# Attention fused with a two-layer MLP: the first pair of token blocks goes through the second weight by plain products

## The chip, the cores and the metric

The kernel runs on one NeuronCore of a Trainium2 chip. The core has a matrix engine (TensorE, in the profile PE, and PEld for its weight loads), three engines for elementwise work (VectorE or DVE, ScalarE or ACT, GpSimd or POOL), a SyncE (SP) that issues transfers, and 16 DMA engines. Every engine works through a queue of its own in program order and waits there for semaphores of the others. The metric is the time of one execution on the device in microseconds: the median of three runs before was 390.96 us (390.53 to 391.64).

## The reference

Softmax attention over 8 batches, 12 heads, 448 tokens, 64 elements a head, and then an MLP with a leaky rectifier over the 3,584 rows of 768 numbers:

```python
scores = scale * np.matmul(q, k.transpose(0, 1, 3, 2))
attn = np.exp(scores - np.max(scores, axis=-1, keepdims=True))
attn = attn / (np.sum(attn, axis=-1, keepdims=True) + 1e-09)
x = np.matmul(attn, v)           # to (3584, 768)
h = x @ w_in                     # w_in: 768 x 2048
g = np.maximum(0.01 * h, h)
out = g @ w_out                  # w_out: 2048 x 768
```

Inputs and output are float32; the kernel multiplies in bfloat16 and sums in float32.

## The kernel before, in words

**Attention.** The 48 pairs of heads (8 batches of 6) are numbered u = 0 to 47. For a pair, q, k and v are loaded by POOL's DMA queue (`load_soft`, L141), cast to bfloat16 (`cast`, L170 and L172, by POOL from u = 4 on), and q and k are transposed: by TensorE up to u = 14 (`transposes`, L254, with a copy by VectorE, L260), later by a DMA transpose on SP (`dma_transposes`, L237). Scores are made in four chunks of 112 keys a pair (L271, two matmuls a chunk), and ScalarE takes the exponential (L280). A *burst* is three chunks, one into each of three PSUM slots. When the four chunks of a pair are done, `rows` multiplies by v (32 matmuls, L765); VectorE then takes the reciprocal of the sums (L771) and multiplies (L772), and SP transposes the result into `xT` (L237). This step of pair u is called *row block u* below. It occupies one of the three slots until L772 has ended.

**MLP.** Tokens are cut into stages of 640, 512, 512, 512, 512, 384 and 512. A stage first makes h (`head` and `neck` for stage 0, `hidden(i)` for the others) and then the output (`second(i)`), two blocks of 128 tokens at a time. `head` takes the first 448 tokens by plain products, `neck` the next 192 (L621, with the rectifier on ScalarE, L648). `hidden` and `second` use Winograd's form of Strassen's scheme: seven products of half matrices in the place of eight, with sums of the operands made beforehand on VectorE and sums of the results afterwards.

**Sums of the operands.** `mix_weights` is a generator that makes the sums of w_out's quarters in four pieces: `t3` (L364) and `t2` (L366) and `t4` (L372) into `w_mix`, and L369, which replaces the right half of w_out's upper rows by right minus left, in place. A `next(outs)` emits one of the 16. Three are taken in `head`, 13 in `neck` by `after`. `mix_w_in` does the same for w_in; its last five steps (L390) are taken in `second(0)`, by `next(ins)`. `mix_h(i, m)` makes, for two of the upper eight row blocks of h, the difference of the two blocks of tokens of each pair into `h_mix` (L435) and adds the lower half of h to the upper half in the second block of the pair, in place (L436). For stage 0 its four calls stand in `after`, behind every second step of `neck`.

**A pair of blocks.** `block_pair(i, c)` is a generator too. It runs seven products of eight matmuls of 384 columns (L535), yielding in the middle of and after each, so that it has 14 steps, x = 0 to 13. Two PSUM banks, `banks`, are used in turn. VectorE sums h in place (L547, L552), copies a bank out (`keep`, L540) or adds it (`join`, L543), and SP stores the block (L330).

**Order of the work.** All of it is emitted in a fixed order, written out by hand. Between the steps of a pair, `place` decides by a clock of its own (`model`) whether a burst or a row block goes in: 0.65 us a half product, 0.78 a burst, 1.08 a row block, 0.8 an exponential; a slot is free when that clock has passed its due time. At steps 1 and 3 no row block is placed (`calm`), since the pair's first sums are then on VectorE. At even steps `advance` emits a DMA transpose of q and k (SP), a cast (POOL), a cast of v, and every second time a load. `plan` has nine bursts in `second(0)`. The sums of x for the next stage (L415) are emitted one a step from 7 us of that clock after the row block that they need, and what is left of them at the end of `second`. `second(0)` begins with 13 row blocks done and must end with 18; the first bursts take their chunks from u = 13.

Of the kernel before, what the change touches and what calls it, by code (L numbers as in the profile page):

```python
# [9 lines left out]
F32 = mybir.dt.float32  # L10
# [6 lines left out]
def kernel(  # L17
# [9 lines left out]
    nc = tc.nc  # L27

    B, H, S, D = q.shape
    DM, DF = moe_w_in.shape  # L30
    P = 128
# [4 lines left out]
    MD = DF // P  # L36
    NW = DM // 2
    NU = B * HP
# [3 lines left out]
    NR = len(cuts) - 1  # L42
    HEAD = S
    need = [HP * -(-t // S) for t in cuts]
# [14 lines left out]
    o_pool = ctx.enter_context(tc.tile_pool(name="o", bufs=3))  # L59
# [6 lines left out]
    banks = [ps_g.tile([P, 4 * P], F32, name=f"g{i}") for i in range(2)]  # L66
# [7 lines left out]
    def next_bank():  # L74

        banks.reverse()
        return banks[1]
# [17 lines left out]
    def place_of(t):  # L95
        return (t + NX - cuts[3]) % NX
# [6 lines left out]
    w_out_sb = w_pool.tile([P, MD, DM], BF16)  # L103
# [3 lines left out]
    h = h_pool.tile([P, MD, (KEEP + 1) * P], BF16, name="h")  # L107
    h_mix = h_pool.tile([P, MH, 2, P], BF16, name="hmix")
# [13 lines left out]
    for t in (w_in_mix, w_mix):  # L122
        t = t.rearrange("p x k n -> p (x k n)")
# [197 lines left out]
    def store(o, t0, cols=slice(0, DM), queues=(nc.sync, nc.sync)):  # L321

        queues = list(queues)
        done = 0
        while done < P:
            b, j = divmod(t0 + done, S)
            so, p = divmod(j, SC)
            n = min(SC - p, P - done)
            dst = out[b * S:(b + 1) * S].rearrange("(p so) n -> so p n", so=NSC)
            queues.pop(0).dma_start(out=dst[so, p:p + n, cols], in_=o[done:done + n, cols])  # L330
            done += n
# [4 lines left out]
    def settle(n=3):  # L336
        while late and n:
            expo(*late.pop(0))
            n -= 1
# [4 lines left out]
    def part(i, m, kks, bank=None):  # L344

        n = HEAD
        at = place_of(0)
        fresh = m not in open_t
        if fresh:
            open_t[m] = next_bank() if bank is None else bank  # L350
        for kk in kks:
            nc.tensor.matmul(
                open_t[m][:, :n], w_in_sb[:, kk, ts(m, P)], xT[:, kk, at:at + n],
                start=(fresh and kk == kks[0]), stop=(kk == KD - 1),
            )

    def mix_weights():

        pieces = [(slice(m, m + 2), slice(MH + m, MH + m + 2)) for m in range(0, MH, 2)]
        left, right = slice(0, NW), slice(NW, DM)  # L360
        for todo in (pieces[:2], pieces[2:]):
            for lo, hi in todo:
                t2, t3 = w_mix[:, 0, lo], w_mix[:, 1, lo]
                nc.vector.tensor_sub(t3, w_out_sb[:, hi, right], w_out_sb[:, lo, right])  # L364
                yield
                nc.vector.tensor_add(t2, t3, w_out_sb[:, lo, left])  # L366
                yield
            for lo, hi in todo:
                nc.vector.tensor_sub(w_out_sb[:, lo, right], w_out_sb[:, lo, right], w_out_sb[:, lo, left])  # L369
                yield  # L370
            for lo, hi in todo:
                nc.vector.tensor_sub(w_mix[:, 2, lo], w_out_sb[:, hi, left], w_mix[:, 0, lo])  # L372
                yield

    def mix_w_in():

# [41 lines left out]
    def spots(i):  # L418

        if i == 0:  # L420
            return 0, [(0, 1), (2, 3)]
        return 0, [(0, 2), (1, 3)] if cuts[i + 1] - cuts[i] == 4 * P else [(0, 1), (KEEP, 2)]

    def token(i, x):

        return KEEP * P if x == KEEP else cuts[i] + x * P

    def mix_h(i, m):

        at = spots(i)[1]  # L430
        step = [max(1, at[-1][y] - at[0][y]) for y in range(2)]
        one, two = (slice(at[0][y], at[-1][y] + 1, step[y]) for y in range(2))
        lo, hi = slice(m, m + 2), slice(MH + m, MH + m + 2)
        t = h.rearrange("p m (c t) -> p m c t", t=P)
        nc.vector.tensor_sub(h_mix[:, lo, :len(at)], t[:, lo, one], t[:, lo, two])  # L435
        nc.vector.tensor_add(t[:, lo, two], t[:, lo, two], t[:, hi, two])  # L436

    def hidden(i):
# [79 lines left out]
    def block_pair(i, c):  # L518
# [67 lines left out]
        store(o2, t0)  # L586
        banks.reverse()

    def head(ins, outs):

        for m in opened:
            part(0, m, (KD - 1,))
        for m in range(MD):
            if m not in opened:
                part(0, m, range(KH))
                for _ in range(2 if 5 <= m < 11 else 0):
                    next(ins)
                for _ in range({13: 1, 15: 2}.get(m, 0)):
                    next(outs)
                yield KH * HEAD / 2400, False  # L600
                part(0, m, range(KH, KD))
            nc.scalar.activation(h[:, m, :HEAD], open_t.pop(m)[:, :HEAD], AX.Prelu, alpha=0.01)
            settle()
            if m == opened[-1]:
                slots.append(idle)
            yield (KH if m not in opened else 1) * HEAD / 2400, True

    def neck(outs):

        n = cuts[1] - HEAD  # L610
        at = place_of(HEAD)
        ms = [x + y for x in range(0, MH, 2) for y in (0, MH)]
        held = {}

        def part2(m, kks):
            fresh = m not in held
            if fresh:
                held[m] = next_bank()
            for j in range(2):
                for kk in kks:  # L620
                    nc.tensor.matmul(  # L621
                        held[m][:, j * n:(j + 1) * n], w_in_sb[:, kk, ts(m + j, P)], xT[:, kk, at:at + n],
                        start=(fresh and j == 0 and kk == 0), stop=(kk == KD - 1), skip_group_check=True,
                    )

        assert all(u == need[1] - 1 for u, _ in owed_x), owed_x
        def after(x):
            for _ in range((4, 4, 3, 2, 0, 0, 0, 0)[x]):
                next(outs)
            if x % 2:  # L630
                mix_h(0, ms[x - 1])

        for m in ms[:2]:
            part2(m, range(KD - 1))
        yield 4 * (KD - 1) * n / 2400, False
        for x, m in enumerate(ms):
            if x < 2:
                assert rows_done >= need[1], rows_done
                settle_x()
                part2(m, (KD - 1,))  # L640
                if x:
                    after(x - 1)
            else:
                part2(m, range(KH))
                after(x - 1)
                yield 2 * KH * n / 2400, False
                part2(m, range(KH, KD))
            nc.scalar.activation(  # L648
                h[:, m:m + 2, HEAD:cuts[1]], held.pop(m)[:, :2 * n].rearrange("p (m t) -> p m t", m=2), AX.Prelu, alpha=0.01
            )  # L650
            settle(1)
            yield 2 * (KH if x > 1 else 1) * n / 2400, True
        model["free"][id(slots[0])] = model["now"] + 1.5
        transposes(NPE - 1, next_slot()[:, 0])
        after(len(ms) - 1)

    def supply(u):
# [246 lines left out]
    def second(i):  # L904

        x_sums = [mix_x_part(i + 1, slice(0, 2)), mix_x_part(i + 1, slice(2, 3))] if i + 1 < NR else []
        fresh, summed = [None, None], [i + 1 == NR] * 2
        left = plan[i]
        for c in range(len(spots(i)[1])):
            for x, _ in enumerate(block_pair(i, c)):  # L910
                if x % 2 == 0:
                    advance()
                if c or x:
                    model["now"] += 0.65
                left -= place(i, left, calm=x not in (1, 3), keen=need[min(i + 2, NR)], cap=NU if all(summed) else need[i + 2])
                if i == 0 and x % 2:
                    next(ins, None)
                for y in range(2):
                    if fresh[y] is None and i + 1 < NR and rows_done >= need[i + 2] - 1 + y:
                        fresh[y] = model["now"] + 7.0  # L920
                for y, todo in enumerate(x_sums):
                    if fresh[y] is not None and fresh[y] <= model["now"] and not summed[y]:
                        summed[y] = next(todo, 0) is not None
                        if not summed[y]:
                            break
        assert left == 0 or chunk == NU * NSC, (i, left)
        assert i + 1 == NR or rows_done >= need[i + 2], (i, rows_done)
        for todo in x_sums:
            for _ in todo:
                pass  # L930

    ins, outs = mix_w_in(), mix_weights()
# [60 lines left out]
```

## Time and profile before

| | |
|---|---|
| three runs, median (lowest to highest) | 390.96 us (390.53 to 391.64) |
| the profiled execution, its own time | 392.0 us |
| its span, first to last instruction | 390.1 us |
| mean granted clock of TensorE | 0.994 |
| `neck`, by TensorE | 62.8 to 73.5 us |
| `second(0)`, by TensorE | 73.9 to 109.4 us |
| first matmul of `hidden(1)` | 110.1 us |

Times in the profile are microseconds from the first instruction, durations of one form in ns. A line of the timeline gives start, duration, engine, line, operation, what it writes and reads, and how often; brackets give how long the engine stood idle before and what ended that. A duration of a merged group of matmuls includes the pipeline's depth, so groups overlap by some 0.15 us: the start of the next group tells the pace.

### The profile page before, as it was taken

What the parts mean: (1) busy time and instruction counts of PE and PEld (TensorE: products, weight loads), DVE (VectorE), ACT (ScalarE), POOL (GpSimd) and SP (SyncE); (2) the same over time, 40 slices, a digit from 0 to 9 for tenths busy, and PEclk for the clock granted to TensorE, in tenths of its full rate; (3) what the DMA queues carried; (4) which work ended last, traced back from release to release, by engine and by line L of the source; (5) the groups of instructions that cost most, each with busy time, mean ns of one, the idle gap of its engine ahead of it and who ended that gap; (6) DMA issues with size and microseconds to landing.
All of it is one profiled execution on the core that took longest, in us unless ns stands there. A gap on an engine that the chain in (4) does not pass through costs nothing.

```text
span 390.1 us, 10005 instructions
## 1 busy us (share of the span) xinstructions
PE 379.3 (97%) x4085; PEld 259.7 (67%) x4085; DVE 235.9 (60%) x494; ACT 265.3 (68%) x391; POOL 138.5 (36%) x222
## 2 busy tenths in 40 slices
PE   8999999799999999999999999999999999999996
PEld 3565657555678655886557865579755796568854
DVE  3663858974465745667458574565745666464853
ACT  6998885547668777587776777667867677708700
POOL 8798621866147142360426404245032000000000
PEclk9999999989999999999999999999999999999999
DMA  9999999999999729993399912999328610321023
GB/s 137 195 200 204 172 187 187 115 126 160 166 129 171 104 49 165 159 173 48 69 157 178 164 25 51 173 182 153 23 58 167 137 27 3 99 61 53 3 76 87
DMA packets 93247, 46.75 MB, mean 120 GB/s; under 512 B 51857, under 2 KB 89873, under 8 KB 93201
## 3 DMA queue, kind: packets, MB, share of 16 engines
q0 software_dynamic: 38224, 22.58, 45.3%
q1 hardware_dynamic: 54912, 23.50, 32.0%
q8 instruction: 32, 0.52, 0.6%
q14 instruction: 15, 0.11, 0.1%
q10 hardware_dynamic: 64, 0.02, 0.0%
HBM read 45.61 MB, written 11.01 MB: 145 GB/s over the span
## 4 chain that ended last, share of the span: by engine, by line
PE 79%; DMA 11%; DVE 5%; POOL 2%; issue 2%; ACT 0%; DVEq 0%; POOLq 0%
PE g L535 32%; PE g L463 14%; PE sc L463 14%; PE sc L765 10%; PE sc L271 8%; DMA w_out_sb<-in_moe_w_out_dram 4%; DMA fk<-in_k_dram 3%; DMA xT<-x 2%; DMA w_in_mix<-in_k_dram 2%; PE g L290 1%; POOL qkb L170 1%; DVE w_mix L372 1%; POOL w_in_mix L141 1%; DVE hmix L435 1%; DVE w_mix L364 1%
## 5 line engine op out<-in xcount | busy, mean ns | idle before, releaser
L280 ACT ACTIVATE e<-sc 112x896 bf16<-112x896 f32 x192 | 163.2, 918 | 52.1 <-PE sc L271 51.9
L535 PEld LDWEIGHTS <-h 128*128 128x128 bf16 x680 | 61.7, 98 | 48.8 <-issue 15.4
L535 PE MATMUL g<-w_out_sb,h 128*128 128x384 bf16 x448 | 85.8, 330 | 0.0
L452 ACT ACTIVATE h<-c 128x512 bf16<-128x512 f32 (+1 forms) x72 | 43.5, 611 | 25.8 <-DVE c L478 16.8
L463 PEld LDWEIGHTS <-w_in_sb 128*128 128x128 bf16 x576 | 54.4, 98 | 6.8 <-issue 0.9
L271 PE MATMUL sc<-qkT 64*128 64x448 bf16 x384 | 50.2, 355 | 3.5 <-DVE x L772 2.7
L170 POOL COPY qkb<-fq 112x512 bf16<-112x512 bf16 x38 | 24.6, 648 | 80.9 <-DMA fq<-in_q_dram 43.5
L765 PEld LDWEIGHTS <-e 112*128 112x128 bf16 x1344 | 46.6, 98 | 8.5 <-ACT e L280 7.0
L765 PE MATMUL sc<-v,e 112*128 112x65 bf16 x1344 | 50.1, 194 | 0.4 <-ACT e L280 0.4
L172 POOL COPY v<-fv 112x512 bf16<-112x512 bf16 x38 | 24.4, 647 | 68.5 <-PE sc L765 68.4
L463 PEld LDWEIGHTS <-w_in_mix 128*128 128x128 bf16 x432 | 41.2, 98 | 4.1
L535 PE MATMUL g<-w_mix,h 128*128 128x384 bf16 (+1 forms) x224 | 41.6, 323 | 0.0
L540 DVE COPY o<-g 128x384 f32<-128x384 f32 x53 | 29.3, 553 | 19.8 <-PE g L535 19.3
L271 PEld LDWEIGHTS <-qkT 64*128 64x128 bf16 x384 | 15.0, 94 | 29.5 <-issue 21.6
L543 DVE TENSOR_TENSOR o<-o,g 128x384 f32<-128x384 f32 x42 | 23.1, 551 | 18.6 <-PE g L535 18.4
L771 DVE RECIPROCAL rec<-sc 112x8 f32<-112x8 f32 x42 | 8.7, 207 | 37.5 <-PE sc L765 37.1
L170 POOL COPY qkb<-fk 112x512 bf16<-112x512 bf16 x38 | 24.3, 639 | 18.5 <-DMA fk<-in_k_dram 18.3
L772 DVE TENSOR_TENSOR x<-sc,rec 112x512 bf16<-112x512 f32 x42 | 29.0, 691 | 1.5
L463 PE MATMUL g<-xT,w_in_sb 128*128 128x256 bf16 (+1 forms) x216 | 28.5, 268 | 0.7 <-DVE o L543 0.7
L463 PE MATMUL sc<-xT,w_in_sb 128*128 128x256 bf16 (+1 forms) x216 | 28.5, 268 | 0.0
L535 PE MATMUL g<-w_mix,hmix 128*128 128x384 bf16 x112 | 21.4, 327 | 0.0
L463 PE MATMUL g<-x_mix,w_in_mix 128*128 128x256 bf16 (+1 forms) x144 | 19.0, 268 | 0.0
(99 smaller groups left out, 460.0 us busy)
## 6 DMA issues: line engine op xcount, KB each, us to landing
fq<-in_q_dram POOLq DMA_DIRECT2D x19, 224.0 KB, 6.5
fk<-in_k_dram POOLq DMA_DIRECT2D x19, 224.0 KB, 7.1
fv<-in_v_dram POOLq DMA_DIRECT2D x19, 224.0 KB, 5.8
w_in_sb<-in_moe_w_in_dram POOLq DMA_DIRECT2D x4, 768.0 KB, 11.4
w_out_sb<-in_moe_w_out_dram POOLq DMA_DIRECT2D x4, 768.0 KB, 19.1
out_dram<-o SPq DMA_DIRECT2D x7, 336.0 KB, 3.8
out_dram<-o SPq DMA_DIRECT2D x8, 288.0 KB, 3.7
out_dram<-o SPq DMA_DIRECT2D x7, 240.0 KB, 3.1
```

Of the source, the lines that this page charges most:

```text
L170: by(qk_sb[u][:, x].rearrange("p so h d -> p h so d"), f)
L172: by(v_sb[u % NV][:, :, :, :D], f)
L271: nc.tensor.matmul(ps[:, j, :S], t[j * D:(j + 1) * D, S + c * SC:S + c * SC + P], t[j * D:(j + 1) * D, :S], start=True, stop=True,)
L280: nc.scalar.activation(e[:, :, c, :], sc_t.pop((u, c))[:SC, :, :S], AX.Exp, scale=scale)
L452: nc.scalar.activation(hs[:, m:m + 2, cols], x.rearrange("p (m t) -> p m t", m=2), AX.Prelu, alpha=0.01)
L463: nc.tensor.matmul(ps[:, j * nh:(j + 1) * nh], w[:, kk, ts(j, P)], x[:, kk], start=(first and j == 0 and kk == 0), stop=(kk == KH - 1), sk ...
L535: nc.tensor.matmul(ps[:, cols], x[:, m], w[:, m], start=(first and m == 0), stop=(m == MH - 1), skip_group_check=True,)
L540: by(o[:, at], ps[:, :NW])
L543: nc.vector.tensor_add(o[:, at], o[:, at], ps[:, :NW])
L765: nc.tensor.matmul(ps[:, j, qc, :], e[:, at:at + P], vt[:, j, c, :], start=(c == 0), stop=(c == NSC - 1),)
L771: nc.vector.reciprocal(rec, ps[:SC, :, :, D:])
L772: nc.vector.tensor_mul(x_t[u].rearrange("p q j d -> p j q d"), ps[:SC, :, :, :D], rec.to_broadcast([SC, 2, NSC, D]))
```

## The change

The first pair of blocks of stage 0 (`plain(0)` is 1) goes through a new generator, `plain_pair`. It computes the two blocks' right halves and then their left halves, each as one chain of 16 matmuls of 384 columns into one of the two banks, copies the bank out by VectorE and stores a block when its second half is there. It has 16 steps, four matmuls each. The stages after 0 and the second pair of stage 0 keep their seven products.

`mix_h(0, m)` leaves the first pair out and works on the second pair alone; its calls move from `neck` to steps 1, 3, 5 and 7 of the plain pair. The four L369 sums move to the end of `mix_weights`, behind an empty step, and are made at steps 9, 11, 13 and 15 of the plain pair, after the products that read the right half. `neck` takes nine sums of w_out in the place of 13. The five L390 steps move to the second pair. Row blocks may be placed at any step of the plain pair.

```diff
             for lo, hi in todo:
-                nc.vector.tensor_sub(w_out_sb[:, lo, right], w_out_sb[:, lo, right], w_out_sb[:, lo, left])
-                yield
-            for lo, hi in todo:
                 nc.vector.tensor_sub(w_mix[:, 2, lo], w_out_sb[:, hi, left], w_mix[:, 0, lo])
                 yield
+        yield
+        for lo, hi in pieces:
+            nc.vector.tensor_sub(w_out_sb[:, lo, right], w_out_sb[:, lo, right], w_out_sb[:, lo, left])
+            yield
...
+    def plain(i):
+
+        return 1 if i == 0 else 0
+
     def mix_h(i, m):
 
-        at = spots(i)[1]
+        c0 = plain(i)
+        at = spots(i)[1][c0:]
...
-        nc.vector.tensor_sub(h_mix[:, lo, :len(at)], t[:, lo, one], t[:, lo, two])
+        nc.vector.tensor_sub(h_mix[:, lo, c0:c0 + len(at)], t[:, lo, one], t[:, lo, two])
         nc.vector.tensor_add(t[:, lo, two], t[:, lo, two], t[:, hi, two])
...
+    def plain_pair(i, c):
+
+        spot = spots(i)[1][c]
+        o = [o_pool.tile([P, DM], F32, name="o") for _ in range(2)]
+        yield
+        for n in range(4):
+            cols, x = slice(NW * (n < 2), NW + NW * (n < 2)), n % 2
+            ps = banks[n % 2]
+            for m in range(MD):
+                if m in (4, 8, 12):
+                    yield
+                nc.tensor.matmul(
+                    ps[:, :NW], h[:, m, ts(spot[x], P)], w_out_sb[:, m, cols], start=(m == 0), stop=(m == MD - 1),
+                )
+            nc.vector.tensor_copy(o[x][:, cols], ps[:, :NW])
+            if n > 1:
+                store(o[x], token(i, spot[x]))
+            if n < 3:
+                yield
...
         def after(x):
-            for _ in range((4, 4, 3, 2, 0, 0, 0, 0)[x]):
+            for _ in range((3, 4, 2, 0, 0, 0, 0, 0)[x]):
                 next(outs)
-            if x % 2:
-                mix_h(0, ms[x - 1])
...
-            for x, _ in enumerate(block_pair(i, c)):
+            whole = c < plain(i)
+            for x, _ in enumerate((plain_pair if whole else block_pair)(i, c)):
...
-                left -= place(i, left, calm=x not in (1, 3), keen=need[min(i + 2, NR)], cap=NU if all(summed) else need[i + 2])
-                if i == 0 and x % 2:
+                left -= place(i, left, calm=whole or x not in (1, 3), keen=need[min(i + 2, NR)], cap=NU if all(summed) else need[i + 2])
+                if whole and x in (1, 3, 5, 7):
+                    mix_h(i, x - 1)
+                if whole and x in (8, 9, 11, 13, 15):
+                    next(outs)
+                if i == 0 and c and x % 2:
                     next(ins, None)
```

## The prediction

> **What bounds the kernel now.** The page's first part comes first: TensorE carries matmuls in 97% of the span, VectorE 60%, ScalarE 68%.
>
> ```profile
> PE 379.3 (97%) x4085; PEld 259.7 (67%) x4085; DVE 235.9 (60%) x494; ACT 265.3 (68%) x391; POOL 138.5 (36%) x222
> ```
>
> So a change pays only where it takes matmuls away or closes a gap between them. The second view is the waits of TensorE from 60 to 112 us, around the changed code:
>
> ```profile
> PE sc L271 <- DVE x L772: 2.7, 1, 2.7
> PE g L463 <- DVE o L543: 0.7, 1, 0.7
> PE sc L271 <- DVE qkT L260: 0.2, 1, 0.2
> ```
>
> The same view from 110 us to the end has one line, that 0.7 us: behind it TensorE waits for nothing, and a shift made before 110 us reaches the end if transfers follow. The third view is TensorE in order of time where the first pair of blocks begins. The columns are start, duration, engine, line, and in brackets the idle time before and who ended it.
>
> ```profile
> 73.91 0.81 PE L535 MATMUL g<-w_out_sb,h 128*128 128x384 bf16 x4
> 74.65 0.36 PE L271 MATMUL sc<-qkT 64*128 64x448 bf16 x2
> 77.69 0.37 PE L271 MATMUL sc<-qkT 64*128 64x448 bf16 x2 [2.67 <-DVE x L772]
> 78.22 0.56 PE L271 MATMUL sc<-qkT 64*128 64x448 bf16 x2 [0.17 <-DVE qkT L260]
> 78.71 3.41 PE L535 MATMUL g<-w_out_sb,h 128*128 128x384 bf16 x12
> 82.05 0.74 PE L271 MATMUL sc<-qkT 64*128 64x448 bf16 x6
> ```
>
> The reader is to see one burst of six score matmuls torn apart. Undisturbed bursts take 0.67 us (82.05 to 82.73) and twelve matmuls 2.06 us (94.87 to 96.93), so 74.65 to 82.05 should last 2.73 us and lasts 7.40: 4.67 us are lost. Only 2.84 of them are idle. The rest is the clock, which the fourth view, busy time by stretch, shows in its third column from the end (granted clock):
>
> ```profile
> 74.54:77.95 3.41, 0.74 (x6) 0.20 (x4) 3.17 (x6) 0.92 (x1) 3.11 (x5) 1.00 1.34 120
> 77.95:81.37 3.42, 3.25 (x13) 1.43 (x12) 2.61 (x6) 1.73 (x2) 0.74 (x2) 0.50 1.77 139
> ```
>
> The fifth view, VectorE in order of time, says why: what frees the score slot is the softmax of row block 12 (reciprocal L771, multiply L772), whose matmuls end at 72.5, and VectorE starts it at 76.71.
>
> ```profile
> 68.98 0.55 DVE L366 TENSOR_TENSOR w_mix<-w_mix,w_out_sb 128x768 bf16<-128x768 bf16 x1
> 69.45 1.91 DVE L369 TENSOR_TENSOR w_out_sb<-w_out_sb 128x768 bf16<-128x768 bf16 x2
> 71.28 2.24 DVE L372 TENSOR_TENSOR w_mix<-w_out_sb,w_mix 128x768 bf16<-128x768 bf16 x2
> 73.44 1.09 DVE L435 TENSOR_TENSOR hmix<-h 128x512 bf16<-128x512 bf16 x1
> 74.64 0.87 DVE L436 TENSOR_TENSOR h<-h 128x512 bf16<-128x512 bf16 x1
> 75.44 0.82 DVE L435 TENSOR_TENSOR hmix<-h 128x512 bf16<-128x512 bf16 x1
> 76.36 0.43 DVE L436 TENSOR_TENSOR h<-h 128x512 bf16<-128x512 bf16 x1
> 76.71 0.20 DVE L771 RECIPROCAL rec<-sc 112x8 f32<-112x8 f32 x1
> 76.94 0.69 DVE L772 TENSOR_TENSOR x<-sc,rec 112x512 bf16<-112x512 f32 x1
> ```
>
> **The change, part by part.**
>
> *Extra matmuls.* Four plain products are 64 matmuls, the seven Winograd products 56. Eight matmuls last 1.30 us in the rows (86.20: 1.40 with the change of shape behind them; the chain has 1.30). All of it is on the path: **+1.30**.
>
> *VectorE's queue ahead of row block 12.* The four L369 sums (1.02 + 1.91 us) and three of the four sums of h (67.71 to 68.98, 73.44 to 76.71: 4.54 us) leave it: 7.5 us, against a lateness of 76.71 - 72.6 = 4.1. What remains, in order: two L372 from 63.9 (1.02), then the sums on the last quarter of w_out, which is the next thing late (its transfer, issued about 41.2, takes 24.5): 65.76 + 0.55, 0.56, 0.96, 0.56, and 2.24 for two L372, ending near 70.7. Row block 12 is then done near 73.6, the transposed q and k (L260, TensorE's part ends 74.07) near 74.8; the burst needs the first at 74.65 and the second at 75.1. The whole loss goes: **-4.67**. The clock is part of it, and here a rule speaks against me. The Trainium skill, "TensorE: Matmul & The Clock Gate", Part 1: the HAM clock gate, has the array fall to half rate after an idle window of about 3.4 us and asks that gaps stay below that; by it a gap of 2.67 us costs its idle 2.84 alone, and the sum below would be 1.83 us worse. The measured stretch decides otherwise: 0.74 us of matmuls in 3.41 were followed by a clock of 0.50.
>
> *The moved VectorE work.* Four L369 sums (0.55 to 1.44 each), four pairs of h sums now on one block instead of two (at most 0.86 + 0.42 by the median rows of before), four copies out of the banks (0.55) lie beside 17 us of TensorE work with three softmax steps of 0.9; at most 16 us in 17, likely 11. A bank is next written 2.6 us after its product ended, so the copies are covered; the sums of w_out are first read in the second pair's fourth product, about 4 us after the last of them is queued. Five L390 sums shift into the second pair (needed by the next stage's fourth product): there they stand where they stood in the first pair, beside half products of 0.65. **0**. Without cover one late copy costs its 0.55.
>
> *Order of bursts and row blocks.* By the planner's own costs (0.65 a half product, 0.78 a burst, 1.08 a row block, exponentials 0.8 each) the burst times stay the same up to the fourth; the first pair has 16 steps for 14, so the fifth burst comes at its step 14 and row block 16 at step 2 of the second pair, not 4. Counted from burst two, both orders have 14 half products, five bursts and three row blocks up to row block 16, 16.32 us in before (82.05 to 98.37). Burst two moves to 73.91 + 0.75 + 0.67 + 2.06 = 77.4, row block 16 to 93.7.
>
> *The end of the stage.* In before the sums of x for the next stage wait in VectorE's queue for the transposed x of row block 16, and a bank's join behind them holds TensorE:
>
> ```profile
> 100.80 5.79 SPq L237 DMA_TRANSPOSE xT<-x  x2
> 109.07 0.53 DVE L415 TENSOR_TENSOR x_mix<-xT 128x512 bf16<-128x512 bf16 x1 [3.21 <-DMA xT<-x]
> 109.52 0.54 DVE L543 TENSOR_TENSOR o<-o,g 128x384 f32<-128x384 f32 x1
> 110.11 0.81 PE L463 MATMUL g<-xT,w_in_sb 128*128 128x256 bf16 x6 [0.69 <-DVE o L543]
> ```
>
> The matmuls ahead of 110.11 began their last group of four (0.65) at 108.60: 0.86 us lost, **-0.86**. In the new order the first of these sums is queued at step 9, ahead of the fifth product's join, so it is product seven that waits. From row block 16 it is ten half products, three bursts, two row blocks to that product's start: 10.88 us, as from 98.37 to 109.25, giving 104.6. The transfer goes out 2.43 us after the row block starts (98.37 to 100.80), at 96.1, or when the cast of k for block 21 (95.2 to 95.8 in before) and its transpose on SP (1.2 to 1.7) let it, 96.9. It lands 8.24 later by the same transfer in before, 5.1 by the median of its kind in this stretch; the join is done 1.06 after landing. Product seven could start at 102.3 at best and 106.2 at worst: a wait of 0 to 1.6 us. I take **+1.2**, between the two issue times, with the landing of the same transfer (its nearest row; queries' transposes just ahead took 8.7 and 9.6).
>
> *Queues moved past.* SP and POOL keep the order of transfers, with one planner step more in the first pair. POOL does not gain what TensorE gains: it waits for landings there. The tightest use is burst nine, whose third score needs block 20's transposed q and k: issued 97.26, landed 9.6 later, used 108.4 in before. Now SP reaches it near 93.3 (k cast at 92.83), landing by 102.9; burst nine is a half product earlier after row block 16, so the need is 93.7 + 10.0 - 0.65 = 103.0: **0**, with 0.1 us to spare. A later landing costs its lateness.
>
> **Sum:** -4.67 + 1.30 - 0.86 + 1.2 = -3.0 us. On the profiled execution: span 390.1 to 387.1 and its own time 392.0 to 389.0. That execution stands 1.0 above the median of the three runs, 390.96, which would become **388.0**.
>
> **The rivals.**
> 1. *No wait at the end* (transfers lighter as SP is ahead of the loads): 1.2 less, 386.8. For: an xT transfer issued at 105.4 landed in 4.1. Against: the 8.2 of the one in question.
> 2. *Transfers don't move.* Row block 16's x lands at 109.05 as in before, because the channel is full (DMA share above 1 there). Product seven then starts at 110.1, the stage ends at 111.4, and an idle stretch of 5.5 us halves the clock for 3.4 us, +1.7: 3.0 us slower, 394.0. It decides from a landing after 107.7, where the gain is gone. Against: in before this transfer left 0.2 us after its multiply, so it is paced by TensorE.
> 3. *The stall stays* (the change doesn't do what it says): VectorE is still behind at 74.65, because POOL's copies beside it stretch its sums (1.44 for 0.55). Gain nil, +1.30: 392.3. Against: 3 us of margin between 70.7 and 73.6.
> 4. *In-place sums hold the plain products*: matmuls of n = 1 on h columns 4 to 7, and of n = 3 on w_out rows 4 to 7, stand behind sums that write other columns of the same rows. Price: softmax step 0.9 and sums 1.28 in one place, 0.55 to 1.44 in the other, 2.7 to 3.6: 391. Against: in before the first product's matmuls ran at 78.71 on rows whose other blocks were summed until 79.50, at the pace of the halved clock and no slower.
>
> **How the numbers follow.** Main case 0.52 (386.9 to 389.4: the wait of 0 to 1.6 and half a microsecond on either side, to which I add 0.4 for one late qkT), rival one 0.26, rival two 0.08, rival three 0.05, rival four 0.06, and 0.03 for losses that cancel. 0.3% is 1.2 us, about what runs of this kernel differ by (390.53 to 391.64). Faster: 0.52 + 0.26 and a little of the rest, 0.80; same 0.08; slower 0.12. The range reaches down to rival one's 386.8 less 0.4, and up to 390.2, where a partial rival two ends.
>
> **What would show it.** TensorE's wait of 2.67 at a score gone, clock 1.0 from 74 to 82; VectorE idle between about 71 and 72.5; 64 matmuls on a new line; burst two near 77.4, row block 16 near 93.7; the next stage's first matmul at 107.1 for 110.11. Wrong, if that matmul comes after 109, if a wait on a transposed q, k or x above 2 us appears before it, or if waits appear after it.

## The result, and the profile after

The changed kernel took 389.38 us (median of 22 runs), the kernel before beside it 392.6 us (22 runs): a ratio of 0.9946, 95% interval 0.9919 to 0.9972. That is 2.1 us (1.1 to 3.2), where 3.0 were forecast. It is faster, as forecast, by about two thirds of the sum. The three runs of before that were shown (median 390.96) lay on the low side: over the 84 executions of before that belong to the experiments below, the mean span is 390.1 us (389.9, 389.9 and 390.2 on the three occasions on which they ran beside other kernels), and a run's time is 1.8 above its span. Ratios and mean spans leave out the executions that took over 1.5% longer than the fastest of the same kernel (5 of these 84, 2 of 34 of the changed kernel, one of 474.7 us of another).

The profiled execution has a span of 387.8 us and its own time 389.6. Its first page line and its waits of TensorE from 60 to 112 us:

```profile
PE 379.8 (98%) x4093; PEld 260.6 (67%) x4093; DVE 234.2 (60%) x489; ACT 265.3 (68%) x391; POOL 142.9 (37%) x222
```

```profile
PE sc L789 <- ACT e L280: 0.4, 1, 0.4
PE g L541 <- DVE o L549: 0.2, 1, 0.2
```

The wait of 2.7 us at a score is gone, and what is left at the end of the stage is 0.2. TensorE in order of time, at the place shown of before (start, duration, line; the plain products are L606):

```profile
75.19 0.81 PE L606 MATMUL g<-w_out_sb,h 128*128 128x384 bf16 x4
75.93 0.74 PE L271 MATMUL sc<-qkT 64*128 64x448 bf16 x6
76.61 2.12 PE L606 MATMUL g<-w_out_sb,h 128*128 128x384 bf16 x12
78.66 0.74 PE L271 MATMUL sc<-qkT 64*128 64x448 bf16 x6
```

The first burst is whole, and from its start to the second burst 2.73 us pass, where before had 7.40. VectorE in order of time says why (L369 here are the sums into `w_mix` that were L372 in before):

```profile
68.16 0.85 DVE L366 TENSOR_TENSOR w_mix<-w_mix,w_out_sb 128x768 bf16<-128x768 bf16 x1
68.93 1.01 DVE L369 TENSOR_TENSOR w_mix<-w_out_sb,w_mix 128x768 bf16<-128x768 bf16 x2
74.07 0.21 DVE L795 RECIPROCAL rec<-sc 112x8 f32<-112x8 f32 x1 [4.12 <-PE sc L789]
74.31 0.69 DVE L796 TENSOR_TENSOR x<-sc,rec 112x512 bf16<-112x512 f32 x1
75.45 0.62 DVE L260 COPY qkT<-sc 128x896 bf16<-128x896 bf16 x1 [0.45 <-PE sc L254]
```

VectorE now waits 4.12 us for row block 12, instead of being 4.1 late. Busy time by stretch shows a clock of 1.00 (third column from the end) where before had 0.50:

```profile
75.20:78.60 3.40, 3.40 (x26) 1.58 (x22) 3.08 (x5) 2.48 (x4) 3.10 (x6) 1.00 1.21 130
78.60:82.00 3.40, 3.40 (x54) 2.25 (x54) 1.54 (x4) 2.86 (x4) 0.68 (x2) 1.00 1.59 142
```

The end of the stage, in the timelines of SP, VectorE and TensorE:

```profile
99.62 2.67 SPq L237 DMA_TRANSPOSE xT<-x  x2
105.16 0.70 DVE L416 TENSOR_TENSOR x_mix<-xT 128x512 bf16<-128x512 bf16 x1 [1.04 <-DMA xT<-x]
106.37 1.46 PE L541 MATMUL g<-w_mix,h 128*128 128x384 bf16 x8 [0.22 <-DVE o L549]
107.92 0.81 PE L469 MATMUL g<-xT,w_in_sb 128*128 128x256 bf16 x6
```

From the first matmul of the stage to the first of the next it is 32.7 us (75.19 to 107.92), 36.2 in before. So this execution shows 3.5 us for the stage, more than the sum's 3.0, and the runs show 2.1. What follows is about that difference. (The span differs by 2.3 only, because this execution reached the stage 1.28 us later. Its clock was halved from 12.18 to 15.59 us and so at 0.91 on the average in the first 15 us, against 1.00 in before. Of the 14 profiles two have such a fall there, and they are the two that reach the stage last, at 74.8 and 75.2 us.)

### The profile page after: what moved, and what is told of

It is laid out like the page before. It is cut to its first block, busy times and chain, and to the rows that moved or that the text cites. A ratio compares the mean times of both kernels' runs of the same rounds, so it can differ in the third digit from the quotient of the medians.

```text
span 387.8 us, 10006 instructions
## 1 busy us (share of the span) xinstructions
PE 379.8 (98%) x4093; PEld 260.6 (67%) x4093; DVE 234.2 (60%) x489; ACT 265.3 (68%) x391; POOL 142.9 (37%) x222
## 4 chain that ended last, share of the span: by engine, by line
PE 92%; DMA 3%; DVE 2%; POOL 1%; issue 1%; ACT 1%; POOLq 0%; DVEq 0%; ACTq 0%
PE g L541 30%; PE g L469 14%; PE sc L469 14%; PE sc L789 11%; PE sc L271 10%; PE g L352 4%; PE g L606 3%; PE g L647 2%; PE g L290 2%; DMA w_in_mix<-in_k_dram 2%; DMA xT<-x 1%; PE g L254 1%; POOL w_in_mix L141 1%; PE sc L352 1%; PE g L317 1%
## 5 line engine op out<-in xcount | busy, mean ns | idle before, releaser
L541 PEld LDWEIGHTS <-h 128*128 128x128 bf16 x632 | 57.1, 98 | 45.0 <-issue 13.3
L541 PE MATMUL g<-w_out_sb,h 128*128 128x384 bf16 x416 | 78.7, 326 | 0.0
L170 POOL COPY qkb<-fq 112x512 bf16<-112x512 bf16 x38 | 26.9, 707 | 72.1 <-DMA qkT<-qkb 32.1
L172 POOL COPY v<-fv 112x512 bf16<-112x512 bf16 x38 | 25.2, 672 | 69.8 <-PE sc L789 69.0
L541 PE MATMUL g<-w_mix,h 128*128 128x384 bf16 (+1 forms) x208 | 38.3, 323 | 0.2 <-DVE o L549 0.2
L546 DVE COPY o<-g 128x384 f32<-128x384 f32 x49 | 27.1, 553 | 18.6 <-PE g L541 18.0
L170 POOL COPY qkb<-fk 112x512 bf16<-112x512 bf16 x38 | 25.1, 660 | 17.3 <-DMA fk<-in_k_dram 17.2
L549 DVE TENSOR_TENSOR o<-o,g 128x384 f32<-128x384 f32 x39 | 21.5, 551 | 15.0 <-PE g L541 14.9
L541 PE MATMUL g<-w_mix,hmix 128*128 128x384 bf16 x104 | 19.9, 326 | 0.0
```

The lines of the kernel that those rows point to most:

```text
L170: by(qk_sb[u][:, x].rearrange("p so h d -> p h so d"), f)
L172: by(v_sb[u % NV][:, :, :, :D], f)
L541: nc.tensor.matmul(ps[:, cols], x[:, m], w[:, m], start=(first and m == 0), stop=(m == MH - 1), skip_group_check=True,)
L546: by(o[:, at], ps[:, :NW])
L549: nc.vector.tensor_add(o[:, at], o[:, at], ps[:, :NW])
```

## The experiments

Ratios are to the kernel before, run beside each kernel on the same chip, with a 95% interval. "Clear" executions are those with a granted clock of at least 0.9975 over the span; one window of 3.4 us at half clock takes it to about 0.995.

### Is the halved clock paid every time?

The kernel before again, and the changed kernel again, without an edit:

> The kernel before, unchanged, to see how its loss at the first pair of blocks differs between executions. Theory A (the halved clock is paid in a part of the executions only, since it depends on how a window of 3.4 us lies to the idle 2.67 us): the granted clock of the runs falls into two groups, about 0.994 and about 1.0, and the second group's spans are about 1.8 us shorter. Theory B (the clock falls every time, the 4.67 us are lost in each execution): no run shows a clock above 0.996. Ratio 1.000 by both.

> The changed kernel again beside the others, to see which of its executions carry a lowered clock and what that costs. Theory A: no clock loss at the first pair in any run; runs with a clock below 0.997 have it from elsewhere, at the start. Ratio 0.992 to 0.995; Theory B: 0.992 or below, as the full 3 us were forecast.

Before again: 391.73 us, ratio 1.0006 (0.9971 to 1.0042). Of the 84 executions of before, 8 are clear, with a mean span of 388.3 us; 50 lie near 0.995 with 389.8, and 20 near 0.991 with 391.2. One lowered window goes with about 1.5 us. Theory B is out, since the clock does escape. Theory A is right that the loss is paid in a part of the executions only, but the clear ones are few, there are more than its two groups, and the step is 1.5 us, not 1.8. The new profile of before shows the same stall with a gap of 2.19 us and the clock halved from 77.45 to 80.86.

After again: 390.07 us, ratio 0.9957 (0.9926 to 0.9987). Of the 34 executions of the changed kernel 21 are clear, with 387.2 us; 10 lie near 0.995, with 389.8, and one near 0.991. Theory A had said that such runs lose their clock at the start alone; two profiles further down show it halved at the end of the stage as well. Theory B's ratio of 0.992 or below wasn't met. The profile of this run has a wait of 0.93 us at product seven of the second pair, against 0.22 in the first profile.

Filling the gap instead of closing it, twelve matmuls on zeros as below, and six in a second kernel:

```diff
-        for a, c in todo:
+        for x, (a, c) in enumerate(todo):
+            if x == 1 and chunk == 54:
+                for _ in range(12):
+                    nc.tensor.matmul(banks[1], warm[:, :P], warm, start=True, stop=True)
             scores(a, c)
```

> The kernel before, with twelve matmuls of 512 columns on zeros (about 2.6 us, their sums overwritten and never read) put in the place of the idle 2.67 us. They remove no wait of VectorE, only the idleness. Theory A: the clock stays at 1.0 through the stage, and the mean gain over before is what the clock costs on the average, 0.3 to 1.5 us (ratio 0.996 to 0.999). Theory B: 1.8 us (0.9954) or more. If the clock falls in spite of the busy array, both are wrong about the cause.

> The kernel before with six matmuls on zeros in place of twelve: half of the idle 2.67 us is filled, about 1.3 us stay, the wait for VectorE is unchanged. Theory (the clock falls when a window of 3.4 us is idle by some share, not when it is idle throughout): the clock falls less often than in before (59 of 66 executions below 0.9975) and about as seldom as with the gap filled (6 of 12): 5 to 8 of 12; ratio 0.997 to 1.000. Rival (any visible gap of over 1 us halves it): 10 or more of 12, ratio 0.999 to 1.003.

Filled: 391.10 us, ratio 0.9983 (0.995 to 1.0016), 6 of 12 clear. Half filled: 391.66 us, ratio 0.9991 (0.9957 to 1.0024), 6 of 12 clear, as its theory had it. In the profile of the half filled gap the burst is held up about as long as in before (2.63 us from its first score to the one that waits, 77.49 less 74.86; 3.04 and 2.55 in the two profiles of before), but TensorE is idle for only 0.86 us of it, and the clock stays at 1.00 (stretches around that burst):

```profile
77.49 0.37 PE L271 MATMUL sc<-qkT 64*128 64x448 bf16 x2 [0.86 <-DVE x L772]
```

```profile
74.80:78.20 3.40, 2.37 (x13) 0.88 (x12) 3.26 (x7) 1.17 (x2) 2.81 (x5) 1.00 0.99 114
78.20:81.60 3.40, 3.40 (x24) 1.61 (x22) 3.19 (x7) 2.22 (x3) 2.36 (x3) 1.00 1.49 135
```

Clear executions go from 8 in 84 to 12 in 24, so the idle stretch is what lowers the clock at this place. The time gained is small and not told from zero by either interval: the mean spans are 389.6 with the gap filled and 390.3 with it half filled, against 390.1. The profile with the half filled gap also has a wait of 2.76 us at the end of the stage, which comes up again below.

### Which of the moved sums closes the wait?

The seven products kept, only the sums of w_out moved:

```diff
-            for lo, hi in todo:
-                nc.vector.tensor_sub(w_out_sb[:, lo, right], w_out_sb[:, lo, right], w_out_sb[:, lo, left])
-                yield
...
+        for lo, hi in pieces:
+            nc.vector.tensor_sub(w_out_sb[:, lo, right], w_out_sb[:, lo, right], w_out_sb[:, lo, left])
+            yield
...
-            for _ in range((4, 4, 3, 2, 0, 0, 0, 0)[x]):
+            for _ in range((3, 4, 2, 0, 0, 0, 0, 0)[x]):
...
-                if i == 0 and x % 2:
+                if i == 0 and c and x % 2:
                     next(ins, None)
+                if i == 0 and c == 0 and x in (4, 5):
+                    next(outs)
+                    next(outs)
```

> The kernel before with its seven products, and only the four sums of w_out's right half moved behind the second product of the first pair (and the five sums of w_in into the second pair, as in the change). The sums of h stay where they were. Theory (it is the length of VectorE's queue, and 2.9 us of the 7.5 are nearly enough against 4.1 us of lateness): the wait at the first burst falls from 2.67 to at most 1 us, the clock stays, the 1.30 us of extra matmuls are not paid: first matmul of the next stage 3 to 4.5 us after a shorter stage, ratio 0.989 to 0.993. Rival (the sums of h alone keep VectorE late): a wait of 1.5 us or more stays, ratio above 0.995.

388.98 us, ratio 0.9919 (0.9876 to 0.9961). The first burst waits 0.17 us, the clock stays at 1.00 around it, and no plain product is needed. But the stage lasts 33.5 us and not the 31.5 that 36.2 less 4.7 would give, because a wait has grown at its end (TensorE, and VectorE ahead of it):

```profile
107.11 0.82 PE L463 MATMUL g<-xT,w_in_sb 128*128 128x256 bf16 x6 [2.04 <-DVE o L543]
```

```profile
106.17 0.43 DVE L415 TENSOR_TENSOR x_mix<-xT 128x512 bf16<-128x512 bf16 x1 [4.66 <-DMA xT<-x]
106.51 0.55 DVE L543 TENSOR_TENSOR o<-o,g 128x384 f32<-128x384 f32 x1
```

The changed kernel with one of the two groups of sums put back, one execution each (in the first the plain products read the replaced right half, so this part of its output is not the reference's):

```diff
@@ sums of w_out back
+            for lo, hi in todo:
+                nc.vector.tensor_sub(w_out_sb[:, lo, right], w_out_sb[:, lo, right], w_out_sb[:, lo, left])
+                yield
...
-                if whole and x in (8, 9, 11, 13, 15):
-                    next(outs)
@@ sums of h back
+            if x % 2:
+                mix_h(0, ms[x - 1])
...
-                if whole and x in (1, 3, 5, 7):
-                    mix_h(i, x - 1)
```

> The changed kernel with the four sums of w_out put back among the other twelve; the plain products then read the replaced right half, so this part of the output is not the reference's. The h sums stay beside the plain pair. Theory (any 4 us off VectorE's queue are enough; the h sums took 4.54): wait at the first burst at most 0.3 us, clock 1.0 in the stage. Rival (the sums of w_out are what counts): 1 us or more of waiting at the first burst.

> The changed kernel with its sums of h, on one block, back behind every second step of the 192 tokens' part. The sums of w_out stay beside the plain pair. Theory: no wait above 0.3 us at the first burst, since 2.9 us of sums of w_out are gone and the h sums are half as long; stage within 0.4 us of the changed kernel's 32.7 to 33.4. Rival (h sums make VectorE late): 1 us or more of waiting.

Neither shows a wait at the first burst, and from it to the second burst 2.73 and 2.87 us pass. So either group alone is enough, as the theory had it; the wait that the rivals named is not there. Yet both executions took as long as before, 392.39 and 392.26 us, and the stage lasts 35.8 and 36.8 us; the second theory had at most 33.8. The end of the stage did that. In the kernel with the sums of h back (TensorE, VectorE, and the stretches):

```profile
107.89 2.72 PE L541 MATMUL g<-w_mix,h 128*128 128x384 bf16 x8 [3.14 <-DVE o L549]
```

```profile
106.52 0.86 DVE L416 TENSOR_TENSOR x_mix<-xT 128x512 bf16<-128x512 bf16 x1 [4.08 <-DMA xT<-x]
107.30 0.54 DVE L549 TENSOR_TENSOR o<-o,g 128x384 f32<-128x384 f32 x1
```

```profile
107.20:110.60 3.40, 2.71 (x9) 1.31 (x9) 2.49 (x6) 0.00 (x0) 3.40 (x5) 0.50 0.49 102
```

Product seven waits 3.14 us for a join that stands in VectorE's queue behind a sum that waits for the transposed x of row block 16; then the clock is at half, so that the product's eight matmuls take 2.72 us in place of 1.46. The other execution has 2.36 us and the half clock too. Their queues of SP, POOL and the late part of VectorE are those of the changed kernel, so its four profiles of this order give 0.22, 0.93, 2.36 and 3.14 us for one and the same wait. This can be where the missing part of the gain goes, in some of the executions. Two tests follow: take the join out from behind the transfer, and make the transfer land earlier.

### Is it the place in VectorE's queue?

```diff
-                        fresh[y] = model["now"] + 7.0
+                        fresh[y] = model["now"] + (7.0 if i else 99.0)
```

With it, the eight sums of x for stage 1 are queued behind the last copy of stage 0. On the changed kernel (twice, on two occasions) and on the seven products with moved sums of w_out:

> The changed kernel with the same late sums of x. Theory: its wait of 0.2 to 0.9 us at product seven goes, stage 32.3 us; ratio 0.992 to 0.995, that is 1.1 to 1.3 us above the seven products with the same edit, which is the price of eight more matmuls. Rival: the wait returns in the next stage, no change against the changed kernel.

> The changed kernel with late sums of x once more, beside the loads' run on one chip. Theory C: ratio 0.991 to 0.994 as in the first run (0.9923), granted clock at or above 0.9975 in two thirds of the executions or more. Rival (the first run was a lucky draw): 0.9945 or above.

> Seven products as before, the four sums of w_out moved (as in the run of that kind), and the eight sums of x for stage 1 queued on VectorE behind the last copy of the stage, not ahead of the joins of products five and six. Theory (the wait of 2.04 us at the end of that run is the order of VectorE's queue: a join stands behind a sum that waits for a transfer): the wait goes, stage 31.2 to 31.8 us, mean 1.5 to 2 us below the run with the moved sums, ratio 0.985 to 0.990. Rival (the next stage needs the transfer just as soon): a wait of 1 us or more appears in the first products of the next stage, and the ratio stays at 0.991 to 0.993.

The changed kernel with late sums: 388.34 us, 0.9923 (0.9897 to 0.995), and 389.08 us, 0.9922 (0.9886 to 0.9958). The wait at product seven is gone in both profiles, and the stage lasts 32.1 us in both. The mean span of the 19 executions is 387.05 against 388.06 of the changed kernel, and 14 of 19 are clear. By this comparison the wait, with the clock behind it, costs the changed kernel 1.0 us on the average (0.3 to 1.8); the intervals of the ratios overlap.

The seven products with late sums: 389.24 us, 0.9942 (0.9913 to 0.9971). The stage is 31.75 us, and the wait at its end is gone. But the ratio is no better than without the late sums (0.9919), and behind the stage this profile takes 280.9 us, where the one with moved sums alone takes 280.0. Visible waits explain 0.43 us of these 0.9: 0.2 for exponentials and 0.21 for a sum of x in the next stage. Neither forecast came true: the theory's ratio was missed, and the rival's wait of 1 us or more in the next stage isn't there. The other half of the 0.9 us stays unexplained.

### Is it the transfer?

The transposed x landed in these profiles at 104.7 to 106.5, at most 0.3 us behind the landing of the load of k for pairs 22 and 23, which POOL had begun to issue up to 1.9 us ahead of it. In the profile of the changed kernel POOL's cast starts when that load lands, 0.2 us ahead of the sum of x that starts at 105.16:

```profile
104.96 0.61 POOL L170 COPY qkb<-fk 112x512 bf16<-112x512 bf16 x1 [1.25 <-DMA fk<-in_k_dram]
```

The loads of q and k for these pairs at the planner's steps 12 and 14, not 8 and 10 (loads behind them move too):

```diff
-        if tick % 2 == 0:
+        if tick % 2 == 0 and tick not in (8, 10):
             x = min(range(3), key=lambda x: to["load"][x])
```

> The changed kernel with the loads of q and k of pairs 22 and 23 issued by the planner's steps 12 and 14, not 8 and 10 (their transfers landed 0.2 us before or after the transposed x in each of the four profiles of this order). The sums of x stay where they are. Theory C (the landing of row block 16's transposed x is set by the loads that the same DMA engines carry, so TensorE's lead becomes a wait of 0.2 to 3.1 us, in part of the executions with the halved clock on top): it lands 5.5 us or less after its issue instead of 5.5 to 7.2, the wait at product seven goes in most executions, ratio 0.990 to 0.994, near the run with late sums. Rival (the loads are not what delays it; SP's issue at 99 is): landing 105 or later, ratio as the changed kernel's, 0.9946 to 0.9957.

> Seven products, the sums of w_out moved, the sums of x late, and the two loads later as well. Theory C: with the transposed x landing sooner the waits of 0.2 us in the next stage go too, and the eight matmuls saved show: ratio 0.986 to 0.990, 1 us or more below the changed kernel with late sums. Rival (TensorE has run into ScalarE's exponentials and the casts, another limit): ratio 0.991 to 0.994, no better than the plain pair.

On the changed kernel: 388.11 us, ratio 0.9890 (0.9861 to 0.9919). Time to landing of the transposed x of row block 16, from the view of that tile, first in the kernel with the sums of h back and then with the later loads:

```profile
L237 SPq DMA_TRANSPOSE xT<-x x1: 1222/1222/1222, 99.2 to 99.2; - x1
DMA to landing us min/median/max: 7.2/7.2/7.2
```

```profile
L237 SPq DMA_TRANSPOSE xT<-x x1: 1981/1981/1981, 97.9 to 97.9; - x1
DMA to landing us min/median/max: 4.2/4.2/4.2
```

It lands at 102.1, and the sums of x, still ahead of the joins, cost nothing (VectorE and TensorE):

```profile
102.69 0.42 DVE L416 TENSOR_TENSOR x_mix<-xT 128x512 bf16<-128x512 bf16 x1
103.05 0.56 DVE L549 TENSOR_TENSOR o<-o,g 128x384 f32<-128x384 f32 x1
104.93 1.46 PE L541 MATMUL g<-w_mix,h 128*128 128x384 bf16 x8
106.23 0.82 PE L469 MATMUL g<-xT,w_in_sb 128*128 128x256 bf16 x6
```

Product seven follows on the product before it, the stage lasts 32.1 us, and the six executions lie within 0.5 us (standard deviation) of 386.3, where the changed kernel's spread by 1.6. The ratio is a little better than the 0.990 forecast. Theory C is borne out in the main: with the loads out of the way the transfer takes 4.2 us, where it took 5.5 to 7.2. But the edit also brought the issue forward, to 97.9 from 98.9 to 99.8, so of the 2.6 to 4.4 us by which x lands sooner 1.0 to 1.9 come from the issue, which the rival had named. One profile doesn't part the two further.

The seven products with late sums and later loads: 387.15 us, ratio 0.9888 (0.9843 to 0.9933), profiled stage 30.7 us and span 384.3. By mean spans it is 0.3 us below the plain pair with later loads (386.0 and 386.3, six executions each). The eight matmuls saved show in the stage, but the ratios of the two kernels can't be told apart. Both beat the kernel before. Against the changed kernel (0.9919 to 0.9972) the interval of the plain pair with later loads just touches and that of the seven products overlaps a little.

## Why the prediction was right or wrong

*Extra matmuls, +1.30.* Right: the matmuls keep their pace (84.88 to 86.94, twelve in 2.06 us as in before), and with waits out of the way the stage takes 32.1 us with the plain pair and 30.7 with seven products.

*VectorE's queue, -4.67.* Right in mechanism and in the profile: VectorE was done 5.3 us ahead of the stage's first matmul (69.9 and 75.2; 3.2 us, 70.7 and 73.9, was worked out), the burst is whole, the clock stays. On the average of the executions it is a little less. The kernel with later loads has no end wait and differs from before by 3.8 us in mean span (390.1 less 386.3, 0.5 either way); with 1.30 paid and 0.86 of the old end wait gone, that leaves 4.2 for the stall, if the later loads do nothing else. The rule in "TensorE: Matmul & The Clock Gate" was weighed and set aside by one row; the new profile of before agrees with that row, the clock halved after a gap of 2.19 us.

*The moved VectorE work, 0.* Right. One sum of h took 2.16 us beside POOL and one of w_out 2.40, both above the rows that the term was added up from (0.43 and 1.44), but no copy was late for TensorE.

*Order of bursts and row blocks.* Right to 0.1 us: taken from the start of the stage, burst two is at 3.47 (worked out: 77.4 less 73.9, 3.5) and row block 16 at 19.8 (worked out: 93.7 less 73.9, 19.8).

*The end of the stage, -0.86 and +1.2.* **This is the step that failed**: the wait of product seven, given as 0 to 1.6 us with nothing for the clock behind it. It was 0.22, 0.93, 2.36 and 3.14 us in four profiles, and in the last two the clock was halved behind it.

Two readings in it were wrong. The first is the issue of the transfer, put at 96.1 to 96.9, which is 22.2 to 23.0 us from the stage's start. It was at 98.9, 99.2, 99.6 and 99.8, or 24.4 to 25.6 from the start. The transpose of block 21 stands ahead of it on SP and waits for POOL's cast of k. In before and in the changed kernel (POOL, then SP):

```profile
95.19 0.62 POOL L170 COPY qkb<-fk 112x512 bf16<-112x512 bf16 x1
```

```profile
93.74 0.62 POOL L170 COPY qkb<-fk 112x512 bf16<-112x512 bf16 x1 [1.72 <-DMA fk<-in_k_dram]
96.53 0.60 POOL L170 COPY qkb<-fk 112x512 bf16<-112x512 bf16 x1
97.16 2.38 SPq L237 DMA_TRANSPOSE qkT<-qkb  x1
```

POOL had waited for the load of k for pairs 20 and 21, so the cast of block 21 did not move forward with TensorE: it started at 95.1 to 97.9 in the four profiles. I had written that POOL doesn't gain what TensorE gains, and then took the cast at its time in before and SP behind it to be in time. (By the rows of before alone, a cast that ends at 95.8 and 1.2 to 1.7 us on SP make 97.0 to 97.5, not 96.9.) Where the cast was as early as in before, in the second profile of the changed kernel, the transpose held SP for 2.98 us, where 1.2 to 1.7 had been reckoned:

```profile
95.78 2.98 SPq L237 DMA_TRANSPOSE qkT<-qkb  x1
98.86 1.23 SPq L237 DMA_TRANSPOSE xT<-x  x1
```

The second is the landing, taken as 8.24 us from the issue because the same transfer in before had it. It took 5.5 to 7.2 us, close behind the load of k each time. The two errors pull against each other, so it is partly luck that +1.2 lies inside what was measured. Counted over executions the wait, with the clock, costs 1.0 us by the kernels with late sums and 1.7 by the one with later loads (388.1 less 386.3; this one may hold other effects of the loads). Nor is the old end wait a fixed 0.86: with the seven products and the sums where they were in before, four profiles show 0.24, 0.69, 0.86 and 2.76 us of idle time there. One profile can't price a wait that varies so.

With 4.2 and 1.7 in the place of 4.67 and 1.2 the sum is -4.2 + 1.3 - 0.86 + 1.7 = -2.1 us. That it meets the measured 2.1 is no test of it, since both numbers are differences of the same mean spans; it says where the missing microsecond can have gone, about half to each term.

*Rivals.* Rival two, transfers that don't move, was half right and had too small a chance at 0.08. From the stage's start row block 16 moved forward by 4.5 to 4.7 us in the four profiles. The landing moved by 5.2 and 4.5 in two of them, but by only 3.1 and 2.3 in the other two, and in these the clock did fall, as that rival said. Rival one, no wait, came near in single executions (0.22 us in the first profile), not on the average. Rivals three and four did not come: no plain product waited for a sum in place.

*The level.* 388.0 was reckoned from a median of three runs that lay 1.6 us below the median of 22.

## What to carry to other kernels

When a stall is taken from the bounding engine, ask for each transfer behind it what it waits for besides that engine; one that lands with another queue's loads keeps part of its time, and the lead turns into a wait. A wait that comes after a transfer should have nothing behind it in an in-order queue that someone else needs: an edit of VectorE's order and one of the order of loads, each alone, brought another 1.0 and 1.7 us beside the change's 2.1 (by mean spans). Before paying for a larger change, move the late work alone: four sums moved closed the same stall without eight extra matmuls, at a ratio of 0.9919 against 0.9946 and 0.9957.

## What the runs showed of the hardware

The clock does not depend on a gap's length alone. It halved for one window of 3.4 us after gaps of 2.19, 2.36, 2.67 and 3.14 us, and did not after one of 2.04 (seven products, moved sums) and one of 2.76 us. The last is in the half filled kernel at the end of the stage:

```profile
110.51 0.81 PE L463 MATMUL g<-xT,w_in_sb 128*128 128x256 bf16 x6 [2.76 <-DVE o L543]
```

The granted clock there is 1.00 up to the end of the span. "TensorE: Matmul & The Clock Gate" (Part 1) says that the window runs freely and isn't reset by the program, and that fits: what counts is how a gap lies in it. In the profile of before the window was 74.54 to 77.95, with matmuls in 0.74 of 3.41 us. If the windows of the half filled kernel's profile are counted on from its first rise of the clock at 6.18 us in steps of 3.413, the gap from 107.75 to 110.51 is cut at 108.57 and leaves each side 43% busy or more; in the four cases that fell, the same count leaves 22% to 36%. That is a reading of six cases, not a measured threshold.

The other profiles bear the count out, and limit it. In all 14 every later change of the granted clock lies a whole number of such steps behind the first rise. After the first 15 us each counted window that TensorE was busy in for 41% or less was followed by half clock (the ends of the kernels, where TensorE runs dry, among them), and none with 43% or more was. But in the first 15 us the clock fell behind windows with 69% (the changed kernel, 8.76 to 12.18) and 67% (the seven products with late sums, 8.20 to 11.62). So the busy share alone does not decide it, and what does at the start was left open.

The same gap can so cost 1.5 us more in one execution than in the next, and a mean over executions is needed to price it.

What was left open: how often the changed kernel's lowered windows come from the end of the stage and how often from the first 15 us, since only profiled executions show the place.
